# Other addresses for two operands of a float32r product, and 512 columns a product in one quarter of it

## The chip, the core and the metric

One core of a Trainium2 chip runs the whole program in one launch. The metric is device time in microseconds (us), lower is better. Engines are named as the profile names them: PE is TensorE (PEld its weight loads), DVE VectorE, ACT ScalarE, POOL GpSimd, SP SyncE.

## The reference

Attention with rotary positions (4 batches, 8 heads, 576 tokens, head size 64), a soft mixture of 8 experts with 4 slots each on its output, and an MLP with squared ReLU on the result of that. The change is in the MLP alone:

```python
def _moe2_ref(x, w_in, w_out):          # x 2304 x 512, w_in 512 x 2048, w_out 2048 x 512
    h = x @ w_in
    r = np.maximum(h, 0.0)
    g = r * r
    return (g @ w_out).astype(np.float32)
```

The input x of this MLP has rank 32 (it is the combination of 32 expert slots), so the kernel first multiplies the slots by w_in and then needs only a short contraction for h. The product `g @ w_out` is the large one: 2304 x 2048 x 512.

## The kernel before, in words

A planner (class Plan) takes operations with a cost and a due time and emits them in an order that it computes from these; the addresses of the buffers and the number of columns of a product do not enter it.

The last 230 us of the program are the MLP (`mlp`, line 1284). Its work is cut into 48 steps, `steps` at line 1369: four quarters q of the 2048 hidden features, in each quarter three groups t of 768 tokens, in each group four blocks fc of 128 features. The first 12 steps are the first quarter, and so on.

For each step `mlp1` (line 1371) makes h for 128 features and 768 tokens with two products of 384 columns (line 1385), ACT takes ReLU, and ACT and DVE square it and split the square into a rounded part and the rest, both float32r. They stand in a *buffer of the squares*, `gts`: four of them in turn, each 128 partitions x 2 x 2 x 384 words, 6,144 bytes in a partition. Lines 1292 and 1293 place them: two behind each other in tEb, one in tEa, one in tO0.

`convert_w_out` (line 1344) makes a *w_out buffer* for two blocks: 128 x 2 x 2 x 512 float32r, 8,192 bytes in a partition, rounded part and rest. These stand in the slots w9, w0, w2, w1 in turn and again w9, w0, w2, w1, so that the first quarter reads w9 and w0, the second w2 and w1, the third w9 and w0, the fourth w2 and w1. The first block pair of a quarter meets the squares in tEb, the second those in tEa and tO0.

`mlp2` (line 1437) multiplies. For each of six groups c of 128 tokens it adds three products (rounded x rounded, rounded x rest, rest x rounded) into bank c, each cut into two of 256 columns by the loop at line 1452; the product is line 1453. The squares are the stationary operand (128 columns), w_out is the moving one. So a step has 36 products of 256 columns: each a weight load of 128 columns and a pass of 256. Over the kernel that is 1,728 products, 432 in a quarter. Between the products of a step stand the two 384-column products of a later step. Twice in the second quarter and twice in the third the 128-column weights of w_in are prepared (`w_prime`, lines 1321 and 1337, products of float32).

Addresses (bytes in a partition, from the program's allocation): the squares stand at 72,672 and 78,816 (tEb), 64,480 (tEa) and 85,472 (tO0), all 224 modulo 256. The w_out buffers stand at 221,088 (w9), 147,360 (w0), 163,744 (w2) and 155,552 (w1), all 160 modulo 256. The slices that a product takes begin at multiples of 512 bytes from there. So moving minus stationary address is 192 modulo 256 in all 1,728 products. In the 384-column products of line 1385 both operands stand at 224 modulo 256: the difference is 0.

In the attention stage the scores are products of 288 columns in float32r, two at a time on 64 rows each (lines 438, 504 and 511): there moving and stationary operands stand at differences of 0, 96, 128 and 224 modulo 256, mixed. Line 638 transposes with 128 columns a piece.

Of the kernel before, what the change touches and what calls it, by code (L numbers as in the profile page):

```python
# [9 lines left out]
F32 = mybir.dt.float32  # L10
F32R = mybir.dt.float32r
# [27 lines left out]
class Plan:  # L39
# [25 lines left out]
    def op(self, engines, fn, due, reads=(), writes=(), kb=None, after=None, spare=None, take=None, give=None, wait=0.0, behind=None, tok=None, mode=None, like=None):  # L65

        i = len(self.ops)
        deps = set()
        for r in reads:
            if r in self.writer:
                deps.add(self.writer[r])
        for w in writes:
            if w in self.writer:
                deps.add(self.writer[w])  # L80
            deps.update(self.readers.get(w, ()))
        if after is not None:
            deps.add(after)
        for b in (behind, like):
            if b is not None and b not in deps:
                deps.add(b)
                self.behind.add((b, i))
        self.like[i] = like
        deps.discard(i)
        self.ops.append((engines, fn, due, sorted(deps), kb, self.SPARE if spare is None else spare, take, give, wait, tok, mode))  # L90
        for r in reads:
            self.readers.setdefault(r, set()).add(i)
        for w in writes:
            self.writer[w] = i
            self.readers[w] = set()
        return i
# [97 lines left out]
def kernel(  # L194
# [20 lines left out]
    pool = ctx.enter_context(tc.tile_pool(name="sb", bufs=1))  # L215
# [6 lines left out]
    WT = 2048  # L222
# [14 lines left out]
    def view(base, at, shape, dt=F32):  # L237
        n = int(np.prod(shape[1:])) * (1 if dt == F16 else 2) // 2
        ap = base[:, at : at + n]
        if dt != base.dtype:  # L240
            ap = ap.bitcast(dt)
        names = "abc"[: len(shape) - 1]
        if len(names) == 1:
            return ap
        return ap.rearrange(
            f"p ({' '.join(names)}) -> p {' '.join(names)}", **{c: shape[1 + i] for i, c in enumerate(names)}
        )
# [50 lines left out]
    def dma(fn, due, kb, reads=(), writes=(), after=None, on="SP", behind=None):  # L298
        return op({on: 0.5}, lambda e: fn(), due, reads, writes, kb=kb, after=after, behind=behind)
# [506 lines left out]
    def tt2_of(slot):  # L806
        tag, size, at_ = TAGS[slot]
        if tag not in tt2:
            tt2[tag] = pool.tile([128, size], F32, tag=tag, name=f"{tag}2")
        return tt2[tag][:, at_:]  # L810

    def claim(slot, *parts):


        fresh[0] += 1
        no = fresh[0]
        olds = {"tEa": gen["E1"], "tEb": gen["E0"] + gen["EX"]}.get(slot) or gen[slot.lstrip("t")]
        held = {}
        box = ring.setdefault(slot, {})
        if slot[0] == "w" and parts[0][1] == F32R:  # L820
            ring[slot] = {}
        out_, at_ = [], 0
        for i, (shape, dt) in enumerate(parts):

            def of(at_=at_, shape=shape, dt=dt):
                if slot in PLACE:
                    base, a = PLACE[slot]
                    return view(base, a + at_, shape, dt)
                if slot in TAGS:
                    return view(tt2_of(slot), at_, shape, dt)  # L830
                if slot[0] == "w" and dt != F32R:
                    if not box:
                        box[0] = pool.tile([128, WT], F32, tag=slot, name=f"{slot}_")
                    return view(box[0], at_, shape, dt)
                if len(parts) == 1:
                    if not held:
                        held[0] = pool.tile(shape, dt, tag=slot, name=f"{slot}_{no}")
                    return held[0]
                if not held:
                    n = sum(int(np.prod(s[1:])) for s, _ in parts)  # L840
                    held[0] = pool.tile([128, n], dt, tag=slot, name=f"{slot}_{no}")
                n = int(np.prod(shape[1:]))
                names = "abc"[: len(shape) - 1]
                return held[0][:, at_ : at_ + n].rearrange(
                    f"p ({' '.join(names)}) -> p {' '.join(names)}", **{c: shape[1 + i] for i, c in enumerate(names)}
                )

            key = ("slot", slot, no, i)
            plan.inherit(key, olds)
            out_.append((of, key))  # L850
            at_ += int(np.prod(shape[1:]))
        gen[slot] = [k for _, k in out_]
        return out_
# [224 lines left out]
    def experts():  # L1078
# [191 lines left out]
        for r in range(4):  # L1270
# [5 lines left out]
            g - 20, [("b", 7)], [("sit", 0), ("sit", 1)], wait=WAIT,  # L1276
        )
        mlp(g + 2, sot, start)


# [3 lines left out]
    def mlp(g, sot, start):  # L1284
# [4 lines left out]
        cv = claim("PX", FLAT)  # L1289
        wfs = claim("A3", HALF, HALF)  # L1290
        cs[0] = claim("A2", COLS, COLS)
        gts = claim("tEb", *[([128, 2, 2, 384], F32R)] * 2) + claim("tEa", ([128, 2, 2, 384], F32R))
        gts += claim("tO0", ([128, 2, 2, 384], F32R))
        ((wst_of, wst_key),) = claim("tO1", ([128, DFF], F32R))
        for n in range(4):
            for h in range(2):
# [140 lines left out]
        def mlp2(n):  # L1437
            q, t, fc = steps[n]
            gt_of, gt_k = gts[n % NG]
            wo_of, wslot = wos[fc // 2]  # L1440
            wo_reads = [("wo", fc // 2, i) for i in range(2)]
            if n == FQ - 1:
                for sl in ("w3", "w4", "w5", "w6", "w7"):
                    sums.extend(claim(sl, *[([128, DM], F32)] * (4 if sl != "w7" else 2)))
            for c in range(6):

                def mm(e, c=c):
                    spare_bank.clear()
                    gt = gt_of().rearrange("p a b t -> p a (b t)")
                    wo = wo_of()  # L1450
                    for i, (x, y) in enumerate(((0, 0), (0, 1), (1, 0))):
                        for z in (slice(0, 256), slice(256, 512)):
                            nc.tensor.matmul(  # L1453
                                BANKS[c][:, z],
                                lhsT=gt[:, x, 128 * c : 128 * c + 128],
                                rhs=wo[:, fc % 2, y, z],
                                start=(fc % FQ == 0 and i == 0 and z.start == 0),
                                stop=(fc % FQ == FQ - 1 and i == 2),
                                skip_group_check=z.start > 0,
                            )  # L1460

                op({"PE": 0.7}, mm, g + n, [(gt_k, c // 3)] + wo_reads, [("b", c)])
                if fc % FQ < FQ - 1:
                    continue
                o_of, o_k = sums[6 * t + c]
                if q == 0:
                    op(
                        {"ACT": 0.5},
                        lambda e, o_of=o_of, c=c: nc.scalar.activation(out=o_of(), in_=BANKS[c], func=AF.Copy),
                        g + n, [("b", c)], [o_k],  # L1470
                    )
                else:
                    op(
                        {"DVE": 0.68},
                        lambda e, o_of=o_of, c=c: nc.vector.tensor_tensor(out=o_of(), in0=o_of(), in1=BANKS[c], op=ALU.add),
                        g + n - 1, [("b", c)], [o_k],
                    )
                if q == NQ - 1:
                    r0 = TT * t + 128 * c
                    dma(  # L1480
                        lambda o_of=o_of, r0=r0: nc.sync.dma_start(out=out[r0 : r0 + 128, :], in_=o_of()),
                        g + n, 262, [o_k],
                    )
            if t == NT - 1 and fc % 2:
                free(wslot, g + n)
# [127 lines left out]
```

## Time and profile before

| | |
|---|---|
| time before, median of 2 runs | 593.69 us (593.42 to 593.97) |
| the profiled execution's own time | 592.18 us |
| its span, first to last instruction | 590.4 us |
| PE busy | 562.1 us, 95% of the span |
| granted clock of PE, mean | 0.994 |
| the four quarters of the MLP's large product | from 361.9 us to the end |

PE busy is the share of time in which at least one product was in flight; products overlap, so that how fast they follow each other is read from the chain of waits (time of a piece divided by its instructions), not from the duration of one. Times in the rows below are us from the span's start.

### The profile page before, as it was taken

What the parts mean: (1) busy time and instruction counts of PE and PEld (TensorE: products, weight loads), DVE (VectorE), ACT (ScalarE), POOL (GpSimd) and SP (SyncE); (2) the same over time, 40 slices, a digit from 0 to 9 for tenths busy, and PEclk for the clock granted to TensorE, in tenths of its full rate; (3) what the DMA queues carried; (4) which work ended last, traced back from release to release, by engine and by line L of the source; (5) the groups of instructions that cost most, each with busy time, mean ns of one, the idle gap of its engine ahead of it and who ended that gap; (6) DMA issues with size and microseconds to landing.
All of it is one profiled execution on the core that took longest, in us unless ns stands there. A gap on an engine that the chain in (4) does not pass through costs nothing.

```text
span 590.4 us, 13397 instructions
## 1 busy us (share of the span) xinstructions
PE 562.1 (95%) x5519; PEld 423.3 (72%) x5519; DVE 406.6 (69%) x853; ACT 269.5 (46%) x475; POOL 217.5 (37%) x172
## 2 busy tenths in 40 slices
PE   1899999999999999999999899999999999999996
PEld 1756565566665666666754337999999999999996
DVE  3687887887787787777455458995594587535553
ACT  1234444444444443453432237876864465443440
POOL 1999999986879677721200000000000000000000
PEclk9799999999999999999999999999999999999999
DMA  9556775566367244036469998421400120000222
GB/s 188 120 124 164 185 193 148 152 175 169 100 174 210 54 100 105 24 95 227 154 226 378 386 392 330 143 81 64 144 1 1 60 84 2 1 1 1 108 108 107
DMA packets 36253, 80.90 MB, mean 137 GB/s; under 512 B 7616, under 2 KB 8032, under 8 KB 35168
## 3 DMA queue, kind: packets, MB, share of 16 engines
q1 hardware_dynamic: 34704, 77.98, 43.2%
q10 hardware_dynamic: 1488, 2.06, 1.8%
q8 instruction: 43, 0.70, 0.5%
q14 instruction: 18, 0.15, 0.1%
HBM read 75.24 MB, written 4.72 MB: 135 GB/s over the span
## 4 chain that ended last, share of the span: by engine, by line
PE 81%; DVE 11%; issue 2%; ACT 2%; DMA 1%; POOL 1%; ACTq 0%; DVEq 0%
PE bank L1453 32%; PE obank L551 11%; PE bank L504 10%; PE bank L572 5%; DVE mcol L449 5%; PE bank L438 4%; PE bank L511 3%; PE obank L1385 3%; PE bank L1239 2%; PE bank L638 2%; PE obank L546 2%; DMA arena<-in_rope_dram 1%; PE bank L1178 1%; PE bank L615 1%; POOL arena L344 1%
## 5 line engine op out<-in xcount | busy, mean ns | idle before, releaser
L523 ACT ACTIVATE tO<-bank 128x576 f32<-128x576 f32 x144 | 90.7, 650 | 114.3 <-PE bank L511 87.3
L344 POOL TENSOR_TENSOR arena<-arena 128x576 f32<-128x576 f32 x90 | 125.6, 1418 | 6.8 <-DMA arena<-in_qk_dram 6.2
L449 DVE TENSOR_REDUCE mcol<-bank 128x2 f32<-128x576 f32 x144 | 103.6, 747 | 14.5 <-PE bank L438 12.3
L1453 PE MATMUL bank<-w,tEb 128*128 128x256 f32 x864 | 106.1, 279 | 0.1
L1453 PEld LDWEIGHTS bank<-w,tEb 128*128 128x128 f32 x864 | 103.3, 188 | 2.3 <-issue 1.2
L551 PE MATMUL obank<-tO,pb 128*64 128x288 f32 x512 | 82.2, 424 | 0.0
L531 POOL TENSOR_TENSOR pb<-tO 128x576 f32<-128x576 f32 x32 | 45.2, 1413 | 51.0 <-ACT tO L523 50.9
L1453 PE MATMUL bank<-w,tEa 128*128 128x256 f32 x432 | 53.5, 279 | 0.0
L1453 PEld LDWEIGHTS bank<-w,tEa 128*128 128x128 f32 x432 | 51.9, 188 | 1.2 <-issue 0.8
L1453 PE MATMUL bank<-w,tO 128*128 128x256 f32 x432 | 51.3, 276 | 0.0
L1453 PEld LDWEIGHTS bank<-w,tO 128*128 128x128 f32 x432 | 50.9, 188 | 0.0
L551 PEld LDWEIGHTS obank<-tO,pb 128*64 128x64 f32 x512 | 28.6, 135 | 26.1 <-issue 16.9
L1396 ACT ACTIVATE pb<-obank 128x384 f32<-128x384 f32 x47 | 21.7, 493 | 42.9 <-PE obank L1385 42.9
L1396 ACT ACTIVATE arena<-obank 128x384 f32<-128x384 f32 x48 | 21.7, 494 | 36.2 <-PE obank L1385 36.1
L572 PE MATMUL bank<-tO,ones 128*32 128x288 f32 x256 | 36.5, 409 | 0.0
L504 PE MATMUL bank<-tEb 64*128 64x288 f32 x180 | 30.8, 339 | 1.4 <-DVE mcol L449 1.4
L438 PE MATMUL bank<-tEb 64*128 64x288 f32 x180 | 27.9, 337 | 2.4 <-DVE mcol L449 2.4
L344 POOL TENSOR_TENSOR tLb<-arena,tEb 128x576 fp32r<-128x576 f32 x20 | 28.2, 1420 | 3.1 <-ACT tEb L374 2.9
L504 PEld LDWEIGHTS bank<-tEb 64*128 64x128 f32 x180 | 16.9, 185 | 16.3 <-ACT tO L523 4.8
L1385 PE MATMUL obank<-x,tO 128*128 128x384 f32 x95 | 27.6, 345 | 0.8 <-DVE tO L1333 0.4
L578 DVE STREAM_TRANSPOSE bank<-bank 128x288 f32<-128x288 f32 x32 | 15.9, 498 | 17.5 <-PE bank L572 17.4
L438 PEld LDWEIGHTS bank<-tEb 64*128 64x128 f32 x180 | 15.8, 184 | 16.4 <-issue 8.6
(302 smaller groups left out, 1066.1 us busy)
## 6 DMA issues: line engine op xcount, KB each, us to landing
arena<-in_qk_dram SPq DMA_DIRECT2D x15, 576.0 KB
arena<-in_qk_dram SPq DMA_DIRECT2D x14, 512.0 KB
pb<-in_v_dram SPq DMA_DIRECT2D x16, 320.0 KB
arena<-in_w_dram SPq DMA_DIRECT2D x8, 512.0 KB
tLb<-in_w_in_dram SPq DMA_DIRECT2D x3, 1024.0 KB
pb<-in_w_in_dram SPq DMA_DIRECT2D x3, 1024.0 KB
w__440<-in_w_dram SPq DMA_DIRECT2D x4, 512.0 KB
w__652<-in_w_dram SPq DMA_DIRECT2D x4, 512.0 KB
```

The costliest lines, as they stand in the source:

```text
L344: ENG[e].tensor_tensor(out=o, in0=x, in1=y, op=how)
L438: nc.tensor.matmul(on_ring(tok)[:, j, 0:HQ], lhsT=x[rows], rhs=hi[rows, 0, HALF[c]], start=(u < BOTH or c == 0), stop=(u < BOTH or c == 1),)
L449: lambda e: nc.vector.tensor_reduce(out=mcol[:, h, :, u], in_=on_ring(tok)[:, :, 0:HQ], op=ALU.max, axis=AX.X),
L504: nc.tensor.matmul(st[:, j, 0:HQ], lhsT=w[rows], rhs=q[y][rows, HALF[c]], start=(i == 0 and (u < BOTH or c == 0)), stop=False,)
L511: nc.tensor.matmul(st[:, j, 0:HQ], lhsT=pick[rows, w : w + 128], rhs=mrow[rows, HALF[c]], start=False, stop=(u < BOTH or c == 1),)
L523: lambda e: nc.scalar.activation(out=pr, in_=on_ring(tok)[:, :, 0:HQ], func=AF.Exp, scale=0.125),
L531: lambda e: nc.gpsimd.tensor_tensor(out=acc, in0=one, in1=pr, op=ALU.add),
L551: nc.tensor.matmul(BANKS[6 + h][o, 0:HQ], lhsT=vr[:, u, j, :], rhs=pr[:, j, :], start=(h == 0 and u == 0), stop=(h == 1 and u == 3))
L572: nc.tensor.matmul(sm[QUAD[2 * j + w], 0:HQ], lhsT=one, rhs=xs_[2 * i + w][:, j, :], start=(i == 0), stop=(i == 1))
L1385: lambda e, i=i, t0=t0: nc.tensor.matmul(BANKS[i][:, 0:384], lhsT=wst_of()[:, 128 * fc : 128 * fc + 128], rhs=cst_of()[:, t0 : t0 + 384], ...
L1396: lambda e, i=i, h=h: nc.scalar.activation(out=rg_of()[:, 0, h], in_=BANKS[i][:, 0:384], func=AF.Relu),
L1453: nc.tensor.matmul(BANKS[c][:, z], lhsT=gt[:, x, 128 * c : 128 * c + 128], rhs=wo[:, fc % 2, y, z], start=(fc % FQ == 0 and i == 0 and z.s ...
```

## The change

Three edits. The slots w0 and w1 get 8 words (32 bytes) more in their first buffer, so that w1 begins 32 bytes later, and w2 to w9 64 bytes later: w_out buffers are then at 224 (w9, w2), 160 (w0) and 192 (w1) modulo 256. In front of the second, third and fourth buffer of the squares 32, 64 and 96 bytes are left: the squares are then at 224 and 0 (tEb), 32 (tEa) and 64 (tO0) modulo 256. And in the second quarter (q equal to 1) line 1452 takes all 512 columns in one product.

```diff
@@ -830,7 +830,7 @@
                 if slot[0] == "w" and dt != F32R:
                     if not box:
-                        box[0] = pool.tile([128, WT], F32, tag=slot, name=f"{slot}_")
+                        box[0] = pool.tile([128, WT + 8 * (slot in ("w0", "w1"))], F32, tag=slot, name=f"{slot}_")
                     return view(box[0], at_, shape, dt)
@@ -1289,8 +1289,8 @@
-        gts = claim("tEb", *[([128, 2, 2, 384], F32R)] * 2) + claim("tEa", ([128, 2, 2, 384], F32R))
-        gts += claim("tO0", ([128, 2, 2, 384], F32R))
+        GT, step = ([128, 2, 2, 384], F32R), lambda n: ([128, 8 * n], F32R)
+        gts = claim("tEb", GT, step(1), GT)[::2] + claim("tEa", step(2), GT)[1:] + claim("tO0", step(3), GT)[1:]
@@ -1449,7 +1449,7 @@
                     for i, (x, y) in enumerate(((0, 0), (0, 1), (1, 0))):
-                        for z in (slice(0, 256), slice(256, 512)):
+                        for z in (slice(0, 256), slice(256, 512)) if q != 1 else (slice(0, 512),):
                             nc.tensor.matmul(
```

Moving minus stationary address modulo 256, and columns of a product, by quarter:

| quarter | w_out in | tEb, first | tEb, second | tEa | tO0 | columns | products |
|---|---|---|---|---|---|---|---|
| before, each | w9, w0, w2, w1 | 192 | 192 | 192 | 192 | 256 | 432 |
| first and third | w9, w0 | 0 | 224 | 128 | 96 | 256 | 432 |
| second | w2, w1 | 0 | 224 | 160 | 128 | 512 | 216 |
| fourth | w2, w1 | 0 | 224 | 160 | 128 | 256 | 432 |

On PE, before, in the second quarter around the first preparation of w_in weights (a row is a run of equal instructions; tEa is the buffer of the squares, w_67 w_out in slot w1, bank_89 to bank_91 pairs of banks, x_22 and tO_52 the operands of line 1385):

```order
L1321 MATMUL obank_93<-arena,sit_125 32x256 x4
L1453 MATMUL bank_89<-w_67_4325,tEa_4175 128x256 x12
L1337 MATMUL obank_93<-pb,gsum 128x256
L1453 MATMUL bank_90<-w_67_4325,tEa_4175 128x256 x12
L1385 MATMUL obank_93<-x_22_3802,tO_52_4041 128x384
L1453 MATMUL bank_91<-w_67_4325,tEa_4175 128x256 x12
L1385 MATMUL obank_92<-x_22_3802,tO_52_4041 128x384
```

The same place in the changed kernel:

```order
L1321 MATMUL obank_93<-arena,sit_125 32x256 x4
L1453 MATMUL bank_89<-w_67_4325,tEa_4175 128x512 x6
L1337 MATMUL obank_93<-pb,gsum 128x256
L1453 MATMUL bank_90<-w_67_4325,tEa_4175 128x512 x6
L1385 MATMUL obank_93<-x_22_3802,tO_52_4041 128x384
L1453 MATMUL bank_91<-w_67_4325,tEa_4175 128x512 x6
L1385 MATMUL obank_92<-x_22_3802,tO_52_4041 128x384
```

A run of 12 products of 256 columns became a run of 6 of 512, at the same place between the other products; there are 36 such runs in the quarter. No instruction of another line changed its place on any engine; on DVE, ACT and SP only buffers' names changed.

## Rows read from the trace of the kernel before

**Rows 1.** The page: busy time of engines, clock by slice, chain by engine and line.

```profile
PE 562.1 (95%) x5519; PEld 423.3 (72%) x5519; DVE 406.6 (69%) x853; ACT 269.5 (46%) x475; POOL 217.5 (37%) x172
...
PEclk9799999999999999999999999999999999999999
...
PE 81%; DVE 11%; issue 2%; ACT 2%; DMA 1%; POOL 1%; ACTq 0%; DVEq 0%
PE bank L1453 32%; PE obank L551 11%; PE bank L504 10%; PE bank L572 5%; DVE mcol L449 5%; PE bank L438 4%; PE bank L511 3%; PE obank L1385 3%; PE bank L1239 2%; PE bank L638 2%; PE obank L546 2%; DMA arena<-in_rope_dram 1%; PE bank L1178 1%; PE bank L615 1%; POOL arena L344 1%
```

**Rows 2.** Windows of the four quarters: length, busy time by engine, clock, DMA.

```profile
core 0: us, PE busy (x) PEld busy (x) DVE busy (x) ACT busy (x) POOL busy (x), PEclk, DMA share, GB/s
361.90:421.50 59.60, 59.19 (x492) 56.38 (x491) 49.84 (x67) 44.15 (x75) 0.00 (x0) 1.00 0.36 119
421.50:477.60 56.10, 56.10 (x478) 54.72 (x477) 35.59 (x50) 32.94 (x55) 0.00 (x0) 1.00 0.11 39
477.60:533.50 55.90, 55.90 (x477) 54.60 (x477) 35.51 (x50) 28.41 (x47) 0.00 (x0) 1.00 0.06 20
533.50:590.40 56.90, 52.32 (x451) 52.12 (x450) 27.05 (x40) 18.69 (x32) 0.00 (x0) 1.00 0.23 84
```

**Rows 3.** Chain in the second quarter: start, length, engine, line, instructions.

```profile
425.94 0.35 PE obank L1385 x2
426.30 4.08 PE bank L1453 x36
...
448.11 0.17 PE obank L1385
448.28 0.57 PE obank L1321 x8
448.85 1.61 PE bank L1453 x12
450.46 0.43 PE obank L1337 x2
450.90 1.41 PE bank L1453 x12
452.31 0.18 PE obank L1385
452.49 1.41 PE bank L1453 x12
```

**Rows 4.** Timeline of products (PE) and weight loads (PEld), one step.

```profile
426.13 4.24 PE L1453 MATMUL bank<-w,tEb 128*128 128x256 f32 x36
...
425.96 4.22 PEld L1453 LDWEIGHTS bank<-w,tEb 128*128 128x128 f32 x36
```

**Rows 5.** Chain in the attention stage.

```profile
196.97 0.55 PE bank L638 x5
...
201.96 0.13 PE bank L438 x2
...
203.80 0.13 PE bank L511 x2
203.93 0.40 PE bank L504 x6
```

**Rows 6.** Chain at the end of the last quarter.

```profile
573.58 12.26 PE bank L1453 x108
585.83 0.02 issue
585.85 0.69 DVE w__1833 L1475
586.54 0.60 DVEq L1609
```

**Rows 7.** Chain ahead of the MLP, lines that read the moved w slots.

```profile
335.18 0.99 PE bank L1178 x8
...
342.16 2.74 PE bank L1239 x24
```

## The prediction

> **What bounds the kernel now.** I read the page first. PE is busy 95% of the span and is 81% of the chain that ended last; line 1453, the product that the change touches, is 32% of that chain [rows 1]. The clock of PE is granted in full from the third slice on [rows 1] and in all four quarters (1.00 in each window, the 2.4 GHz level) [rows 2], so that 256 columns alone are 256/2.4 = 106.7 ns, and 512 are 213.3.
>
> The windows then tell who sets the time in the MLP. In the second quarter PE is busy 56.10 of 56.10 us while DVE has 35.59 and ACT 32.94; the third is alike [rows 2]. Whatever a product gains or loses there goes to the end of the kernel one for one: the last piece of the chain is 108 products in a row, with 0.69 us of DVE and the output behind them, which stay [rows 6].
>
> The chain gives the pace. A step's 36 products take 4.08 us, 113.3 ns each, 6.7 more than their columns [rows 3]; in the second quarter nine steps are of this kind, one is 4.20, and the two with weight preparation have runs of 12 in 1.41 us, 117.5 ns each [rows 3]. So the same products at the same addresses already run at two paces. A pair of the 384-column products is 0.35 us, 175 ns each where the columns are 160: 15 more [rows 3]. The timeline shows the weight loads of a step spread over the whole of it, 4.22 us beside 4.24 of products [rows 4]: each load runs under the product ahead of it, so two reads of SBUF by PE run side by side, and their addresses could matter.
>
> **The change, part by part.** *Columns.* 432 products of 256 columns leave the second quarter, 216 of 512 come. A pair cost 2 x 113.3 = 226.7 ns. No row has a float32r product of 512 columns, so it is bounded. From below: line 1337 is float32 and runs its 256 columns as two records; 0.43 us for the two is 215 ns each, nearly bare 512/2.4, with a 128-column weight load under each [rows 3]. That gives 216 x (215 - 226.7) = -2.5 us. From above: 128 columns more, from 256 to 384, cost 175 - 113.3 = 61.7 ns instead of 53.3 [rows 3]; 128 more again give 236.7, or +2.2 us. I take the 384-column row by the column, since it is the widest float32r product in the trace: 175/384 x 512 = 233.3 ns, 216 x 6.7 = **+1.4 us**.
>
> A rule on this: the Trainium skill, "TensorE: Matmul & The Clock Gate", section "Back-to-back issue gap", puts a warm product at N/2.4 + 2.5 ns. That is 215.8 ns for 512 columns and would make this term -2.4 us. The trace does not agree with it here: it would be 109.2 for 256 columns against 113.3 measured, and 162.5 for 384 against 175 [rows 3]. The measured excess grows with the width, so the sum goes by the row.
>
> *Addresses.* 1,296 products of 256 columns in the other quarters go from a difference of 192 to 0, 224, 128 and 96 (or 160 and 128), 324 of them to 0. No row has this product at another difference. From below: five 128-column transposes in 0.55 us are 110 ns each, where 128 columns alone are 53, so they are as fast as weight loads follow each other [rows 5]; 1,296 x (110 - 113.3) = -4.3 us. From above: the slower pace in the trace, 117.5 ns, is +5.4 us [rows 3]. Farther: the 384-column products have a difference of 0 and an excess of 15 ns; put on 256 columns that is 121.7 ns, +10.8 us [rows 3]. The nearest rows on addresses alone are those of the attention stage: its float32r products of 288 columns go by pairs at differences of 0, 96, 128 and 224, and a pair is 0.13 us on each of the three lines (0.40 for three pairs) [rows 5]. Four differences, one pace: I take **0**, and count the 15 ns of the 384 columns as width, not as address, for it cannot be both.
>
> *The 384-column products.* Under the second of a pair lies the load of the next step's squares, whose difference goes from 0 to 0, 224, 192 or 160. 48 pairs, at most the 15 ns of excess either way: 0.7 us. I take 0.
>
> *The other buffers.* Slots w1 to w9 move by 32 or 64 bytes for their whole life, so expert weights are read from there by lines 1178 and 1239: 8 records in 0.99 us, 24 in 2.74, together 3% of the chain at most [rows 1, 7]. A 4% change of pace would be 0.7 us; taken as 0, since these are float32, like line 1337, which shows next to no excess. Loads into them have no place on the chain in the MLP's last three quarters, where DMA is busy 6 to 23% of the time [rows 2]. ACT and DVE write and read the moved squares with the same instructions; if one became some per cent slower, some 20 us of idle time in each of the two middle quarters cover it [rows 2], and without that cover 4% of DVE's 35.59 us would be 1.4 us a quarter.
>
> *Sum.* +1.4 us on the profiled execution's 592.18 us is 593.6. The median of the runs shown, 593.69, stands 1.5 us above that execution, so I forecast **595.1 us** for the runs: no change within 2%, which is about what a measurement of this kernel can tell from no change (11.9 us).
>
> **The rivals.** *The wide product hides its weight load.* Weight loads of 128 columns follow each other at 110 ns [rows 5] and a 256-column product leaves 106.7, so 113.3 could be the pace of loads, and with 512 columns this limit is gone. For it: line 1337 at 215 and the transposes at 110. Against it: the 384-column product also has room for its load and is at 175, not at 160 [rows 3]. It gives -2.5 us, 591.2. This is where the skill's rule above would land, too. Chance 0.25.
>
> *The new differences take collisions away.* Then the 6.7 ns over the bare columns are two reads meeting, and at most differences they no longer do: 110 ns in 1,296 products and 215 in 216, -6.8 us, 586.9; half of it if only some of the four buffers gain, 590.3. For it: two paces at one difference show that something besides width and load sets the pace. Against it: one pace at four differences in the attention stage. Chance 0.13.
>
> *The new differences collide more.* The two reads meet more often and the pace falls to the one that the trace has in the steps with preparation, 117.5, and stays: +5.4 us, and the wide products cost twice that, 235, +1.8: 600.9. Chance 0.16. In the far form the excess of 15 ns at difference 0 was an address after all and holds for all four buffers: 121.7 and 243.4, +10.8 + 3.6 = +14.4, 608.1. This is slower by over 2% from the point at which a former product costs 11.9 us / 1,728 = 6.9 ns more, 120.2 on average; only difference 0, a quarter of them, has a row that speaks for that. Chance 0.04. Both forms and the one before have a rule against them: the Trainium skill, "SBUF — State Buffer", section "SBUF: two separate sides", gives PE separate read ports for moving operand and weights and says that they never wait. By that rule the addresses are worth nothing, and the trace neither shows nor excludes it: the excess of 6.7 to 15 ns is there, its cause is not [rows 3].
>
> **How the numbers follow.** My forecast (columns cost a little, addresses nothing) 0.42, at 593.7 to 595.9 between the row at 226.7 and that at 236.7; hidden load 0.25; fewer collisions 0.13; more 0.16, far form 0.04. Gains and losses in different buffers can also cancel, which lands in the forecast's stretch. The range reaches down to half of the gain by addresses and up to just short of the full slower pace: 588.5 to 600.0. It leaves out the far form, about half of the case of more collisions and the full case of fewer: 0.18. Faster by over 2% (under 581.8) is beyond every bound above, 0.02; slower (over 605.6) is the far form and a little, 0.05; within 2% 0.93.
>
> **What would show it.** In the chain of the second quarter a step is 18 products: 4.20 us by my step, 3.87 if the load is hidden, 4.26 at the upper bound. In the first, third and fourth quarters a step of 36 stays at 4.08 us in all four buffers of the squares by my second step; it is 3.96 with fewer collisions, 4.23 with more. If the four buffers differ among themselves, addresses matter and my zero is wrong whatever the total says; if the first buffer of tEb alone is slower, it is difference 0. The pieces of line 1385 should stay at 0.35 a pair. I would be wrong altogether if the second quarter's window were not full of PE any more, or its clock no longer 1.00.

## The result: slower by 1.2%, most of it in the quarters whose products only changed address

The changed kernel takes 601.12 us (601.11 to 601.12, 2 runs) against 593.69 before: a ratio of 1.0121, 95% interval 1.0097 to 1.0145. That is within 2%, but clear of no change, and 1.1 us above my range.

The windows of the four quarters in the changed kernel, in the columns of [rows 2]:

```profile
core 0: us, PE busy (x) PEld busy (x) DVE busy (x) ACT busy (x) POOL busy (x), PEclk, DMA share, GB/s
364.30:425.30 61.00, 60.92 (x493) 58.45 (x493) 50.20 (x67) 44.55 (x75) 0.00 (x0) 1.00 0.35 117
425.30:482.00 56.70, 56.70 (x261) 45.67 (x261) 35.28 (x50) 32.56 (x54) 0.00 (x0) 1.00 0.11 38
482.00:540.00 58.00, 58.00 (x477) 56.68 (x477) 35.75 (x50) 28.28 (x47) 0.00 (x0) 1.00 0.06 19
540.00:599.30 59.30, 54.76 (x452) 54.55 (x450) 27.08 (x40) 18.68 (x32) 0.00 (x0) 0.99 0.22 81
```

PE is still full and its clock still granted in full (0.99 in the last window, where it falls after PE's last product), and DVE and ACT work as long as before: it is PE's own pace that fell. The first quarter went from 59.6 to 61.0 us, the second, with the 216 wide products, only from 56.1 to 56.7, the third from 55.9 to 58.0. The last, to the end of its last product, went from 52.3 (533.5 to 585.83) [rows 2, 6] to 54.8 (540.0 to 594.77). Together some 6.5 us, about 5.8 of them in the three quarters that kept 256 columns. The medians of the runs differ by 7.4.

The chain in the changed kernel, in the columns of [rows 3]: the second quarter's first four steps, then four of the third, then the end. The four steps of a group read the first and second buffer of tEb, tEa and tO0.

```profile
425.45 4.12 PE bank L1453 x18
429.57 0.35 PE obank L1385 x2
429.92 4.20 PE bank L1453 x18
434.11 0.35 PE obank L1385 x2
434.46 4.21 PE bank L1453 x18
438.67 0.35 PE obank L1385 x2
439.02 4.20 PE bank L1453 x18
...
482.16 4.32 PE bank L1453 x36
...
486.84 4.25 PE bank L1453 x36
...
491.45 4.27 PE bank L1453 x36
...
496.07 4.32 PE bank L1453 x36
...
581.96 12.81 PE bank L1453 x108
594.77 0.02 issue
```

A step of 18 wide products takes 4.10 to 4.21 us, 228 to 234 ns each. A step of 36 in the third quarter, at differences 0, 224, 128, 96, takes 4.32, 4.25, 4.27, 4.32, which is 118 to 120 ns a product. In the kernel before, every step of this quarter without preparation took 4.08, as this one:

```profile
482.20 4.08 PE bank L1453 x36
```

In the last 108 products DVE is busy for only 4.09 us and ACT for 1.58, the same as in the kernel before, and the pace is as low: 12.81 / 108 = 118.6 ns, against 113.5 before [rows 6].

The profiled spans differ by 8.9 us, 2.4 more than these quarters. Nearly all of that part arises at 45 to 52 us in the attention stage, where the instructions are the same: PE's products start at the same times in both traces from 29 to 44 us, within 0.04 us, and 2.31 us apart at 52. There the changed kernel's execution was granted 0.56 and 0.50 of the clock (the 1.2 GHz level; windows 45 to 48 and 48 to 52). PE's work ahead of it does not tell the two executions apart: it was busy 3.10 of the 4 us before 44, and 3.12 in the kernel before, which kept its full clock there. The execution of before had its half-clock stretch at 20 to 28 us (0.54 and 0.60 in the windows 20 to 24 and 24 to 28); it held products back by up to 1.05 us, which were made up by 28 us. The first product of line 1453 starts between 361.9 and 365.5 us in the fourteen profiles of this case, and runs of the kernel before lie between 592.5 and 596.3 us. So in the experiments I read the MLP in the trace, where a step repeats within 0.01 us.

### The profile page after: what moved, and what is told of

The parts are those of the page before. It is cut to its first block, busy times and chain, and to the rows that moved or that the text cites. A ratio compares the mean times of both kernels' runs of the same rounds, so it can differ in the third digit from the quotient of the medians.

```text
span 599.3 us, 12965 instructions
## 1 busy us (share of the span) xinstructions
PE 572.1 (95%) x5303; PEld 421.5 (70%) x5303; DVE 406.4 (68%) x853; ACT 269.4 (45%) x475; POOL 217.4 (36%) x172
## 4 chain that ended last, share of the span: by engine, by line
PE 82%; DVE 11%; issue 2%; DMA 2%; POOL 1%; ACT 1%; ACTq 0%; SPq 0%; DVEq 0%
PE bank L1453 34%; PE obank L551 11%; PE bank L504 10%; PE bank L572 6%; DVE mcol L449 5%; PE bank L438 4%; PE bank L511 3%; PE obank L1385 3%; PE bank L638 2%; PE bank L1239 2%; PE obank L546 2%; DMA arena<-in_rope_dram 1%; PE bank L1178 1%; PE bank L615 1%; POOL arena L344 1%
## 5 line engine op out<-in xcount | busy, mean ns | idle before, releaser
L1453 PE MATMUL bank<-w,tEb 128*128 128x256 f32 (+1 forms) x756 | 109.4, 299 | 0.1
L1453 PEld LDWEIGHTS bank<-w,tEb 128*128 128x128 f32 x756 | 100.6, 189 | 6.2 <-issue 1.2
L1453 PE MATMUL bank<-w,tEa 128*128 128x256 f32 (+1 forms) x378 | 55.0, 300 | 0.0
L1453 PE MATMUL bank<-w,tO 128*128 128x256 f32 (+1 forms) x378 | 53.5, 298 | 0.0
L1453 PEld LDWEIGHTS bank<-w,tEa 128*128 128x128 f32 x378 | 50.2, 188 | 3.1 <-issue 0.8
```

What stands on the lines that cost most here:

```text
L1453: nc.tensor.matmul(BANKS[c][:, z], lhsT=gt[:, x, 128 * c : 128 * c + 128], rhs=wo[:, fc % 2, y, z], start=(fc % FQ == 0 and i == 0 and z.s ...
```

## Experiments

In all tables and texts "difference" is moving minus stationary address of line 1453 modulo 256. Three edits recur: bytes ahead of the squares, bytes ahead of the operands of line 1385 (x1 is the moving one, tO1 the weights), and the columns.

**1. The columns alone.**

```diff
-                        for z in (slice(0, 256), slice(256, 512)):
+                        for z in (slice(0, 256), slice(256, 512)) if q != 1 else (slice(0, 512),):
```

> The kernel before with one part of the change: 512 columns in the second quarter, addresses as before (difference 192 everywhere). Theory A, the addresses are the cost: the first, third and fourth quarters keep 4.08 us a step, and a step of 18 wide products takes between 4.08 and 4.20 us; total -0.5 to +1.5 us against the kernel before. Theory B, the wide products upset the pace of what comes after them too: the third and fourth quarters are at 4.26 to 4.32 as in the changed kernel; total +5 to +6 us.

Measured: ratio 1.0016 (0.9996 to 1.0035). In the chain, a step of the second and one of the fourth quarter:

```profile
440.84 4.20 PE bank L1453 x18
...
553.43 4.08 PE bank L1453 x36
```

Theory A. 4.20 / 18 = 233.3 ns: the price of a wide product was right to the digit. The wide products slow the 256-column ones a little beyond their quarter, one step at 4.24 and one at 4.11, then 4.08 is back. From first to last product of line 1453 the MLP grew by 1.25 us.

**2. The addresses alone.** The two address edits of the change, without the third.

> The change without its wide products: the new addresses, 256 columns in all quarters. Theory A (addresses): steps of 36 at 4.25 to 4.32 us in every quarter, the second too, total +5.5 to +8 us against the kernel before, so no better than the changed kernel. Theory B (wide products): steps stay at 4.08, total within 1 us of the kernel before.

Measured: ratio 1.0133 (1.0108 to 1.0157). Steps of the second quarter, at differences 0, 224, 160, 128:

```profile
426.18 4.31 PE bank L1453 x36
...
430.85 4.26 PE bank L1453 x36
...
435.46 4.28 PE bank L1453 x36
...
440.10 4.27 PE bank L1453 x36
```

Theory A again: the MLP grew by 7.82 us, more than in the changed kernel (6.52). At the new addresses the wide products win back 1.3 us; at the old ones they cost that much. The two parts do not simply add.

**3 and 4. A map by 32 bytes,** with w_out in its old place and 512 columns in the second quarter. The edit of the squares in the second map; the first map has 0, 32, 64 and 96 bytes (`step` counts words):

```diff
-        gts = claim("tEb", *[([128, 2, 2, 384], F32R)] * 2) + claim("tEa", ([128, 2, 2, 384], F32R))
-        gts += claim("tO0", ([128, 2, 2, 384], F32R))
+        GT, step = ([128, 2, 2, 384], F32R), lambda n: ([128, n], F32R)
+        gts = claim("tEb", step(32), GT, step(8), GT)[1::2] + claim("tEa", step(48), GT)[1:] + claim("tO0", step(56), GT)[1:]
```

> w_out stays where it was; the four buffers of the squares are put 0, 32, 64 and 96 bytes farther, so that the differences are 192, 160, 128 and 96; the second quarter has 512 columns, the others 256, so each difference is read at both widths. Theory A1, the difference modulo 256 decides and 192 alone has the regular pace: the first buffer of tEb keeps 4.08 us a step, the three others take 4.25 to 4.32. Theory A2, it is the new place of w_out that costs: all four at 4.08. Theory A3, the farther from 192 the slower: 4.08, then rising step by step to about 4.3.

> As the run before with the squares 128, 160, 192 and 224 bytes farther: differences 64, 32, 0 and 224. Theory A1: all four at 4.25 to 4.32 us for 36 products of 256. Theory A2 (place of w_out): 4.08. Theory A3 (distance from 192): 64 and 32 are the slowest, 0 and 224 come down toward 4.15. At 512 columns my rule of the 384-column row says 233 ns, 4.20 us for 18, whatever the difference; if the address decides there as well, the four differ by more than 0.1 us.

The fourth quarter of the first map, differences 192, 160, 128, 96:

```profile
541.11 4.08 PE bank L1453 x36
...
545.53 4.23 PE bank L1453 x36
...
550.11 4.27 PE bank L1453 x36
...
554.73 4.32 PE bank L1453 x36
```

Of the second, the wide steps at 32, 0, 224, 64, then the fourth quarter at 64, 32, 0, 224:

```profile
427.47 4.19 PE bank L1453 x18
...
432.00 4.09 PE bank L1453 x18
...
436.44 4.19 PE bank L1453 x18
...
440.98 4.20 PE bank L1453 x18
...
537.27 4.24 PE bank L1453 x36
...
541.86 4.21 PE bank L1453 x36
...
546.41 4.31 PE bank L1453 x36
...
551.07 4.26 PE bank L1453 x36
```

Theory A1, nearly: 192 alone has 4.08, the seven others 4.21 to 4.32. A2 falls (w_out did not move), and A3 too, for there is no order by distance. At 512 columns the map differs: 192 is at 4.20 there (run 1) and 0, at 4.09, is the fast one. (The very first wide step, at 64, took 4.13, the later one 4.20.)

**5. Squares and w_out moved together.** All four `step`s 32 bytes, and a pad of 32 bytes ahead of the w slots.

> Squares and w_out both 32 bytes farther than before, so every address differs but moving minus stationary is still 192 in all 1,728 products; 256 columns. Theory R, the difference decides: 4.08 us a step in the second to fourth quarters, as before. Theory P, the places themselves decide (the squares at 224 or w_out at 160): 4.22 to 4.32 a step.

```profile
446.40 4.24 PE bank L1453 x36
...
456.74 4.11 PE bank L1453 x36
...
466.94 4.11 PE bank L1453 x36
...
471.39 4.24 PE bank L1453 x36
```

My theory R failed as put: the difference is 192 everywhere, and most steps are at 4.24, which is 117.8 ns, close to the second pace of [rows 3]. But a step right behind one with preparation is at 4.11. The starts of its products in the trace show why: the first five or so follow each other at 114 to 120 ns, the rest at 113 to 114. So one difference has two paces, and a step does not choose by its own addresses alone.

**6, 11 and 12. Finer.** Bytes ahead of the squares 4, 8, 16, 240; 80, 144, 176, 208; 48, 112, 248, 252.

> w_out as before, the four squares 4, 8, 16 and 240 bytes farther: differences 188, 184, 176 and 208; 256 columns. It asks how near to 192 the regular pace reaches. Theory L, what meets are lines of 16 or more bytes: 188 and 184 keep 4.08 us a step or nearly, 176 and 208 do not (4.2 or more). Theory W, word by word: only 192 itself has 4.08, all four are between 4.15 and 4.32. Theory B, a broad valley around 192: all four at 4.08 to 4.15.

> Differences 112, 48, 16 and 240 at 256 columns (squares 80, 144, 176 and 208 bytes farther). If 192 is the one difference with a regular pace, all four are at 4.2 to 4.32 us a step; if there are more such differences, one or more of these is at 4.1 or below, and a kernel with that one is the candidate to beat the kernel before.

> Differences 144, 80, 200 and 196 at 256 columns (squares 48, 112, 248 and 252 bytes farther). As the run before for 144 and 80. 200 and 196 are the near side of 192 that was not tried: if 4 bytes are enough to lose the regular pace on the other side as well, both are at 4.2 to 4.3; if the regular pace reaches above 192 and not below, they are at 4.08 to 4.12.

A step of 36 in the fourth quarter, read in the same way (us):

| difference | 188 | 184 | 176 | 208 | 112 | 48 | 16 | 240 | 144 | 80 | 200 | 196 |
|---|---|---|---|---|---|---|---|---|---|---|---|---|
| step | 4.26 | 4.26 | 4.27 | 4.24 | 4.31 | 4.21 | 4.22 | 4.26 | 4.31 | 4.25 | 4.24 | 4.30 |

Theory W: 4 bytes off 192, on either side, and 4.08 is gone. Of the 20 differences tried none but 192 has it, so none of them offered a faster kernel.

The table has the value that most steps show, but 192 is not the only difference with more than one pace. In run 11 the step at 112 takes 4.21 when it is the first of the third or fourth quarter, and 4.31 otherwise:

```profile
541.67 4.21 PE bank L1453 x36
...
559.98 4.31 PE bank L1453 x36
```

At 160 a step takes 4.22 or 4.23 in run 3, but 4.27 behind a step with preparation, and 4.28 in the changed kernel. None of these paces comes down to 4.08.

In these maps the 384-column products kept their place, so whenever the squares moved, their address relative to those products moved along. One step separates the two: the fifth of the third quarter, in the changed kernel and in run 3. In both it reads the unmoved first squares of tEb, behind the unmoved products of line 1385 and a step of w0 at difference 96; only w9, its own w_out, stands 64 bytes farther in the changed kernel. So its own difference is 0 there and 192 in run 3:

```profile
500.73 4.32 PE bank L1453 x36
```

```profile
501.92 4.09 PE bank L1453 x36
```

So a step's own difference is enough to lose 4.08. Whether one of the other 19 could have a fast pace behind other products is not shown. Nor is 192 modulo 512: by the addresses in bytes, 192 was 448 modulo 512 in every run.

**7. The 384-column products at 192,** everything else as before.

```diff
-        ((cst_of, cst_k),) = claim("x1", ([128, NTOK], F32R))
+        _, (cst_of, cst_k) = claim("x1", ([128, 48], F32R), ([128, NTOK], F32R))
```

> The kernel before with the moving operand of the 384-column products 192 bytes farther, so that it, too, is 192 from its own weights and from the squares loaded under it (both were 0). Theory R (the difference decides, also at 384 columns): a pair of line 1385 falls from 0.35 to about 0.33 us (the excess of 15 ns goes to 7), 96 products x 8 ns = -0.8 us, and the pieces of the first quarter, where such products stand between groups of six, get shorter too; total -1 to -2 us. Theory V (my prediction's: the excess grows with the columns, not with the address): 0.35 a pair, total unchanged within 0.5 us.

Measured: ratio 1.0000 (0.9981 to 1.0018).

```profile
446.06 0.34 PE obank L1385 x2
446.40 4.08 PE bank L1453 x36
...
454.61 0.17 PE obank L1385
454.78 1.36 PE bank L1453 x12
```

In between: a pair went from 0.35 to 0.34, some 5 ns a product where theory R wanted 8 (its first product now takes 170 ns from start to start instead of 175), and the last run of a step with preparation is at 1.36 / 12 = 113 ns again instead of 117.5. The MLP is 0.97 us shorter than before in the trace, the shortest of all; the runs cannot tell that from no change.

**8. 512 columns at difference 0 in all quarters.** All `step`s 192 bytes, and 512 columns for every q.

> 512 columns in all four quarters at difference 0 everywhere (squares 192 bytes farther). In the run with differences 64, 32, 0 and 224 the wide products at 0 went at 4.09 us a step twice and all the others at 4.13 to 4.20. Theory S, each width has its own difference with a regular pace, 192 at 256 columns and 0 at 512: 4.09 us a step in all quarters, total within 1 us of the kernel before. Theory U, those two steps were chance: 4.19 to 4.21 a step, some 0.12 x 48 = 5 to 6 us above the kernel before.

Ratio 1.0009 (0.9990 to 1.0028); in the fourth quarter

```profile
541.59 4.11 PE bank L1453 x18
```

Theory S: 4.11 a step (228 ns), not 4.20. So each width has its own good difference among those tried, and the MLP is as long as before within 0.2 us.

**9 and 10. Entry or place?** "Entry" means the products that PE runs just before a step. These two runs bear on what run 5 left. Run 9 is run 5 with the operands of line 1385 32 bytes farther as well. Run 10 leaves squares and w_out where they were before and moves only the operands of line 1385:

```diff
-        ((cst_of, cst_k),) = claim("x1", ([128, NTOK], F32R))
+        _, (cst_of, cst_k) = claim("x1", ([128, 56], F32R), ([128, NTOK], F32R))
-        ((wst_of, wst_key),) = claim("tO1", ([128, DFF], F32R))
+        _, (wst_of, wst_key) = claim("tO1", ([128, 56], F32R), ([128, DFF], F32R))
```

> Squares, w_out and both operands of the 384-column products 32 bytes farther than before: every address of these streams differs by the same 32, every difference is as in the kernel before. In the run with squares and w_out alone 32 farther, steps were 4.24 us although their difference was 192, and 4.11 behind the preparation of w_in weights. Theory E, at 192 there are two paces (113.3 and 117.8 ns) that keep themselves up, and the difference met on entry from the 384-column products decides which: all entries are as before, so 4.08 a step. Theory P, places themselves decide (squares at 0, w_out at 192 modulo 256 are bad ones): 4.24.

> Squares and w_out exactly as in the kernel before; only the two operands of the 384-column products stand 224 bytes farther (32 less modulo 256), so that on entry to a step the differences are those of the run with 4.24. Theory E: steps at 4.24 us though nothing about their own products changed, 4.1 behind the preparation; second to fourth quarter some +5 us, total +4 to +7. Theory P: 4.08 a step, total as before.

Run 9, with every address of run 5:

```profile
541.22 4.08 PE bank L1453 x36
```

Run 10, with the large products' addresses of the kernel before; ratio 1.0092 (1.0063 to 1.0121). The first line is the step behind the first preparation:

```profile
458.11 4.24 PE bank L1453 x36
...
544.02 4.25 PE bank L1453 x36
...
548.61 4.24 PE bank L1453 x36
...
580.77 12.73 PE bank L1453 x108
```

Theory E in the main, in both. In run 9 not one of the streams is where it was and the pace is back; in run 10 not one byte of line 1453's operands moved and 117.8 ns a product came, even over the last 108 in a row (12.73 / 108 = 117.9). So a shift of everything by the same 32 bytes does not matter; relative addresses do, and at 192 those of the products ahead decide which of two paces a step falls into. One part of the forecast failed: behind the preparation run 10 has 4.24, not the 4.1 of run 5. Which relation counts is open, too: run 10 changed two at once, that of x1 to the squares that are loaded under the second 384-column product, and that of w_out to the weights of line 1385 that are loaded under the last product of the step before. Run 7 moved x1 alone, by 192 bytes, and kept 4.08.

## Why the prediction was wrong, point by point

*What bounds it:* right. PE stayed full, and what its products lost, 6.5 us from the first to the last, reached the end of the kernel.

*Columns, +1.4 us:* right in the price. 233.3 ns forecast, 233.3 measured in run 1; the MLP grew by 1.25 us there. The Trainium skill's N/2.4 + 2.5 ("TensorE: Matmul & The Clock Gate", section "Back-to-back issue gap", there the gap of an isolated product), 215.8 ns, was met at no difference (227 to 234). In the changed kernel the second quarter grew by only some 0.6 us, since at difference 0 the wide products are faster (4.10 and 4.12 a step) than at 192; at 224, 160 and 128 they are not (4.20 and 4.21).

*Addresses, 0:* **the step that failed.** The 1,296 products took some 5.8 us more, 4.5 ns each. I set this to 0 by the rows of the attention stage, four differences at 0.13 us a pair [rows 5]. Those rows cannot bear it. Printed to 0.01 us, 0.13 is known to 4%, and 4% of a product is what was at stake (113.3 to 118). Nor is there one pace: by the starts of the products in the same trace, most pairs of line 504 take 126 to 137 ns from start to start (whether by address, no run shows). And 192 is not among those differences: I compared four others with each other, at another width, while the kernel before sat on the one exception of its own. At 256 columns, too, the 19 other differences are alike within 3%.

*The far end, 121.7 ns:* not reached; the slowest steps are at 120.

*The rivals.* The hidden load (0.25) and the fewer collisions (0.13) are refuted by the runs: no step of wide products came under 227 ns each, and no step of 36 under 4.08 us. "The new differences collide more" came true in its size, at 0.16: 600.9 forecast, 601.1 measured, with 117.5 for the narrow products against 118 to 120 and 235 for the wide ones against 228 to 234. That the totals agree to 0.2 us is luck: it put 5.4 on the narrow products and 1.8 on the wide ones, where the trace has 5.8 and 0.6, and the medians of the runs carry about 1 us more than the MLP. The row that spoke for it was in front of me, 12 products in 1.41 us at an unchanged address [rows 3]: a pace that can be lost without any change of address can be lost by one. I read it as the upper bound and should have read it as the likely state once the fast one is left. Its mechanism I had only half. That two reads meet is not shown; shown is one regular pace, 113.3 ns, that of the 20 differences tried only 192 had, and that is lost there too behind some products. Against it I held a rule (the Trainium skill, "SBUF — State Buffer", section "SBUF: two separate sides": two read ports of PE that never wait) and concluded that addresses are worth nothing. That conclusion does not hold in run 10, where 36 products with unchanged operands take 4.24 instead of 4.08 us; whether the ports wait, no run shows.

*The other buffers, 0, and the 384-column products, 0:* right in their own time. Pairs stayed at 0.35, DVE's work in the second quarter was 35.28 against 35.59 us, and from 52 us to the MLP, where the moved slots are read, the two traces drift apart by only 0.1 us. What I did not ask is whether the 384-column products set the pace of what follows them, as in run 10.

*The range.* Its lower end, 588.5, is not the half gain that the text names (590.3); nothing hangs on it, since the time came out above.

What stays open is why a pace hangs on relative addresses at all. The weight load that runs under each product is the natural other party [rows 4], and run 10 shows that what ran just before matters; that it is the load's read was argued, not shown, since none of the runs took the load away. Open, too, are the relation to the products ahead that decides, and the other paces at 112 and 160.

## What to carry to other kernels

When a stream of equal products runs at one exact pace and the same stream elsewhere at another, the pace may be a state that can be lost, as here: before moving any of its buffers, write down moving minus stationary address and keep it, and look at the products ahead of the stream as well, since in run 10 moving their operands alone was enough. A "no difference" between rows counts only if the rows are printed finely enough to show the effect at stake, and if the present case is among them. Read such an effect in the steps of the trace: a step repeats to 0.01 us, while whole runs here spread over 4 us.

## What the runs showed of the hardware that I had not expected

- float32r products of 128 x 256 by 128 columns ran at 113.3 ns at one relative address of the two operands (192 modulo 256) and at 117 to 120 at the 19 others tried, 4 bytes to either side included.
- At 192 there are two paces, 113.3 and 117.8 ns, each kept over 36 products and both over a last 108 (the kernel before and run 10). Which one comes changed when only the two 384-column products ahead of each step had their operands moved. In run 5 some steps pass from the slow to the fast one within their first few products. 112 and 160 have two paces as well (4.21 and 4.31 us a step in run 11; 4.22 and 4.27 in run 3).
- The good difference depends on the width: at 512 columns 228 ns at difference 0 and 233 at 192 (runs 8 and 1).
- The stretch at half clock (0.50 to 0.60 granted) fell at 20 to 28 us in one execution and at 45 to 52 us in another of the same instructions. The second cost 2.3 us of span; the first held products back by up to 1.05 us, which were made up by 28 us.
